# Five small padding tiles in a window-attention and two-MLP kernel: where the operands of its matrix products begin

## The chip, the cores and the metric

The kernel runs on one core of a Trainium2 chip. The metric is the device time of one execution in microseconds (us). Three executions were timed, and their median counts. TensorE multiplies; its two kinds of instruction stand in the rows as PE (the product, MATMUL) and PEld (the load of the stationary operand, LDWEIGHTS). DVE is VectorE, ACT ScalarE, POOL GpSimd. On-chip memory (SBUF) has 128 partitions; an address below is a byte offset in a partition.

## The reference

```python
# q, k, v: (4, 8, 576, 64); moe w_in (512, 2048), w_out (2048, 512), alpha (2048,); moe2 the same shapes
scores = scale * q @ k.T                      # with a bias -slope[h] * (i - j)
scores = where((i - j >= 0) & (i - j < 128), scores + bias, -1e9)
attn = softmax(scores) @ v                    # window of 128 keys
x = attn.transpose(0, 2, 1, 3).reshape(2304, 512)
h = x @ w_in;  g = max(h, 0) + alpha * min(h, 0);   x = g @ w_out
h = x @ w_in2; g = h * sigmoid(1.702 * h);          out = g @ w_out2
```

All in float32.

## The kernel before

TensorE works on the 4-byte type float32r. To keep float32 accuracy every operand a is split into a high part ah and a rest al, and a product a·b becomes three: ah·bh, ah·bl, al·bh, which add up in PSUM. Every one of them has a stationary operand of 128 partitions x 128 columns, which a LDWEIGHTS loads, and a moving operand of 256, 288 or 512 columns, which the MATMUL streams.

The program runs through five stretches.

- Start: first heads of the attention, and decoding of the first MLP's weights.
- Attention beside the first MLP. Tokens come in blocks of 256. `m1_h` (L579) multiplies a chunk of `w_in` (tiles wh, wl; stationary) with the tokens (tiles xh, xl; moving), 12 products of 256 columns for each of 16 hidden chunks and each of 7 blocks. `m1_o` (L625) multiplies `w_out` with the activations gh, gl, again 12 products for each chunk and block. Between them stand the small products of the attention: scores (L428, L429: stationary q, moving kh, kl), transposes (L492) and values (L530: stationary vp, moving pth, ptl), of 64 to 256 columns.
- The last two blocks go through the same two lines together, with 512 columns (the branch `k == KM`).
- The first product of the second MLP (L787), by a seven-product scheme on half matrices, with 288 columns.
- The second product of the second MLP (L884, `o_mm`), by a seven-product scheme too. Here the activations are stationary (tiles oh, ol) and the weights move (wh, wl), with 256 columns. It runs over 36 units (`quads`, a block of tokens and a pair of hidden chunks); unit number n keeps its activations in one of three tile pairs by n % 3: `oh0` on the left side of SBUF, `oh1` and `oh2` on the right side. A unit of a 512-token block has 42 products (7 x 2 x 3), one of the 256-token block 21.

The order of work is written out by hand in the lists of steps; the tile framework places tiles and semaphores. SBUF is filled from both ends by stacks of pools: a pool on the left side begins where the one opened before it ends, one on the right side ends where the one before it begins. A tile's address follows from the sizes of the pools opened before it and not from anything in its own line. The weight tiles (wh, wl) lie in a left pool opened early, at multiples of 256 bytes. Columns of 128 elements are 512 bytes wide, so all 128-column pieces of a tile have the same address modulo 256.

Of the kernel before, what the change touches and what calls it, by code (L numbers as in the profile page):

```python
# [11 lines left out]
F32 = mybir.dt.float32  # L12
F32R = mybir.dt.float32r
# [8 lines left out]
P = 128  # L22
# [47 lines left out]
def tile_window_attention__then__two_mlps(  # L70
# [20 lines left out]
    dram = ctx.enter_context(tc.tile_pool(name="dram", bufs=1, space=bass.MemoryType.DRAM))  # L91
    psh = ExitStack()
    ps_h = psh.enter_context(tc.tile_pool(name="ps_h", bufs=2, space=PSUM, side="right"))

    alph = const.tile([P, NF], F32, name="alph")
    beta = const.tile([P, NF], F32, name="beta")
# [32 lines left out]
    def w_load(i):  # L129
        layer, f, part = chunks[i]  # L130
        src = ((w_in1, w_out1), (w_in2, w_out2))[layer][part]
        s = wstage.tile([P, DM], I64, tag="ws", name="ws")
        nc.sync.dma_start(out=s, in_=src[f])
        wst[i] = s
# [92 lines left out]
    def w_out_diffs(p, half):  # L227
        c = DM // 2
        if half == 0:
            w0, w1 = wf.pop(("o", 2 * p)), wf.pop(("o", 2 * p + 1))  # L230
            t = stage_f32("sc").rearrange("p (i c) -> p i c", i=4)
            b11, b12, b21, b22 = w0[:, :c], w0[:, c:], w1[:, :c], w1[:, c:]
            tt(t[:, 0, :], b12, b11)
            tt(t[:, 2, :], b22, b12)
            wf["d", p] = t, b21, b22
        else:
            t, b21, b22 = wf.pop(("d", p))
            tt(t[:, 1, :], b22, t[:, 0, :])
            tt(t[:, 3, :], b21, t[:, 1, :])
            nc.sync.dma_start(out=wt2d[p], in_=t)  # L240

    def w_out_load(p):
        w = p2["wo"].tile([P, 2, DM], F32, tag="wo", name="wo")
        nc.sync.dma_start(out=w, in_=wo2d[p])
        if p < NPR - 2:
            t = stage_f32("st").rearrange("p (i c) -> p i c", i=4)
        else:
            t = p2["wo"].tile([P, 4, DM // 2], F32, tag="wo", name="wu")
        nc.sync.dma_start(out=t, in_=wt2d[p])
        wf["w", p] = w, t  # L250
# [54 lines left out]

    ps_o = ExitStack()
    pso = ps_o.enter_context(tc.tile_pool(name="ps_o", bufs=1, space=PSUM, side="right"))
    p1 = ExitStack()
    ring = p1.enter_context(tc.tile_pool(name="ring", bufs=1, side="right"))
    gp, gt, xsp = {}, {}, {}  # L310
# [8 lines left out]
    ap_ = at.enter_context(tc.tile_pool(name="att", bufs=1))  # L319
# [4 lines left out]
    ident = ap_.tile([P, P], F32, name="ident")  # L324
    relt = ap_.tile([P, 2 * P + 192], F32, name="relt")
    xps = ap_.tile([P, 320], F32, name="xp")
    ar = {x: ap_.tile([P, c], F32R, name=x) for x, c in (("q", 384), ("kh", 448), ("kl", 448))}

    af = ExitStack()
    apf = af.enter_context(tc.tile_pool(name="attf", bufs=1))  # L330
# [5 lines left out]
    def a_parts():  # L336
        af.close()
        pool = at.enter_context(tc.tile_pool(name="attr", bufs=1))
        for x, c in (("pth", 704), ("ptl", 640)):
            ar[x] = pool.tile([P, c], F32R, name=x)  # L340
        for i in range(2):
            ar["v", i] = pool.tile([P, 4, P], F32R, name=f"vp{i}")
        for x in ("pth", "ptl"):
            nc.gpsimd.memset(ar[x].bitcast(F32)[:, 384:448], 0.0)
# [308 lines left out]
    def x_load(j, c, key=None):  # L653
        r = stage_f32("xr", TB)
        done = 0
        while done < TB:
            i, o = divmod(j * TB + done, T1)
            m = min(T1 - o, TB - done)
            nc.sync.dma_start(out=r[:, done : done + m], in_=x2d[i][:, c, o : o + m])
            done += m  # L660
        xr[j, c if key is None else key] = r
# [366 lines left out]
    n = H + 2  # L1028
# [41 lines left out]
    halves, n = [], 2 * (H + 2)  # L1070
# [4 lines left out]
    for s, (k, f) in enumerate(steps):  # L1075
        n = H + 2 + s // 2
# [92 lines left out]
    def run():  # L1169
        while todo:  # L1170
            todo.pop(0)[2]()

    def task(fn, dve=0.0, act=0.0):
        todo.append((dve, act, fn))

    def dec_scale(f):
        task(lambda: w_scale(3 * NF + f), act=1.3)

    def dec_add(f):
        task(lambda: (w_shift(3 * NF + f), w_add(3 * NF + f), w_split(3 * NF + f)), 1.1)  # L1180

    def dec_tasks(i):
        task(lambda: w_scale(i), act=1.3)
        task(lambda: (w_shift(i), w_add(i), w_split(i)), dve=1.1)

    def x_tasks(j, cc):
        task(lambda: x_a(j, cc), 0.9, 0.4)
        task(lambda: (x_t12(j, cc), x_d3(j, cc), x_d4(j, cc)), 0.9, 0.65)
        task(lambda: x_lo(j, cc), 1.2)

    def win_tasks(p):
        box = []
        task(lambda: (box.extend(w_in_parts(p)), box[0]()), 1.3, 0.6)
        task(lambda: box[1](), 1.1, 0.4)
        task(lambda: box[2](), 0.4, 1.0)
        task(lambda: box[3](), 1.2)
# [19 lines left out]
    for d in range(NS // 2 + 1):  # L1216
        j, q = divmod(2 * d, NPR)
        q //= 2
        for i, (name, k) in enumerate(slots):
            s = 2 * d + k  # L1220
            if s < 0 or s >= NS:
                continue
            if (d, i) == (1, 0):
                run()
                for k in (2, 1):
                    w_load(W1 + NF - k)
                dec_tasks(W1 + NF - 2)
                win_tasks(6)
                dec_tasks(W1 + NF - 1)
            if (d, i) == (2, 0):  # L1230
                win_tasks(7)
            if j < NJ - 1:
                if (q, i) == (2, 2):
                    for c in (0, 2):
                        x_load(j + 1, c)
                if (q, i) == (2, 8):
                    x_tasks(j + 1, 0)
                if (q, i) == (3, 0):
                    for c in (1, 3):
                        x_load(j + 1, c)  # L1240
                if (q, i) == (3, 4):
                    x_tasks(j + 1, 1)
                if (q, i) == (3, 6):
                    for cc in range(2):
                        x_load(j + 1, cc + 2, f"b{cc}")
            if j in (1, 2):
                f = 2 + 4 * (j - 1) + q
                if i == 0:
                    dec_scale(f)
                if i == 4:  # L1250
                    dec_add(f)
                if i == 8 and f % 2:
                    task(lambda f=f: w_out_diffs(f // 2, 0), 0.85)
                    task(lambda f=f: w_out_diffs(f // 2, 1), 0.85)
                if i == 6 and f < 9:
                    w_load(3 * NF + f + 1)
            if (j, q, i) == (0, 3, 12):
                w_load(3 * NF + 2)
            if j == NJ - 1:
                if (q, i) == (1, 0):  # L1260
                    run()
                    px0.close()
                    p2["oh", 0] = ctx.enter_context(tc.tile_pool(name="oh0", bufs=1))
                    p2["wo"] = ctx.enter_context(tc.tile_pool(name="wo", bufs=2))
                if q and i in (0, 7):
                    w_out_load(2 * (q - 1) + i // 7)
                if q and i in (6, 9):
                    wout_tasks(2 * (q - 1) + (i - 6) // 3)
                if (q, i) == (1, 12):
                    o_load(*quads[0])  # L1270
                if (q, i) == (3, 0):
                    task(lambda: o_split(*quads[0]), 2.4, 2.0)
            h_mm(s, name)
            late.append(lambda s=s, name=name: h_post(s, name))
            if len(late) > 1:
                late.pop(0)()
            if (d, i) == (0, 2):
                for cc in range(2):
                    x_b(0, cc)
                for cc in range(2):  # L1280
                    x_b_lo(0, cc)
            if q == 0 and 0 < j < NJ:
                f = {0: (x_b_lo, 0), 1: (x_b_lo, 1), 2: (x_34, 3), 3: (x_34_lo, 3), 7: (x_34, 4), 8: (x_34_lo, 4)}.get(i)
                if f:
                    f[0](j, f[1])
            if q == 3 and j < NJ - 1 and i == 12:
                run()
                x_b(j + 1, 0)
            if q == 3 and j < NJ - 1 and i == 13:
                x_b(j + 1, 1)  # L1290
            credit = [min(c + 0.8 - t.get(name, 0.0), 2.4) for c, t in zip(credit, (PD, PA))]
            while todo and all(c >= min(x, 2.4) for c, x in zip(credit, todo[0][:2])):
                x = todo.pop(0)
                credit = [c - y for c, y in zip(credit, x[:2])]
                x[2]()
# [6 lines left out]
    p2["gs"] = ctx.enter_context(tc.tile_pool(name="gs", bufs=2, side="right"))  # L1302
    psh.close()
    p2["pr"] = ctx.enter_context(tc.tile_pool(name="ps_r", bufs=1, space=PSUM))
    for i in (1, 2):
        p2["oh", i] = ctx.enter_context(tc.tile_pool(name=f"oh{i}", bufs=1, side="right"))
    p3["o"] = ctx.enter_context(tc.tile_pool(name="ob", bufs=2, side="right"))
# [71 lines left out]
```

## Time and profile before

| | us |
|---|---|
| median of three runs | 915.97 (915.3 to 917.12) |
| span of the profiled execution, first to last instruction | 913.5 |
| median less span: what lies around the span | 2.5 |
| PE busy in the span | 896.6 (98%) |
| PEld busy | 861.0 (94%) |
| DVE busy | 715.3 (78%) |
| ACT busy | 582.7 (64%) |

The profile is of one execution; its own time is the span plus what lies around it, and 2.5 us is put for that, from the median. A MATMUL's busy time is longer than the distance to the next one, since products overlap in the pipeline; what a product costs in a full stream is the distance from its start to the next start, called its spacing below.

### The profile page before, as it was taken

The page shows a single profiled execution, that of the slowest core. Times are in us where ns is not written, and L with a number is a line of the kernel's source. Part 1 is how long each engine was busy: PE and PEld are TensorE (multiplying, and loading weights), DVE is VectorE, ACT ScalarE, POOL GpSimd, SP SyncE. Part 2 cuts the span into 40 slices and gives each one's busy share as a digit, 9 for nine tenths or more (in the row PEclk, how much of TensorE's full clock was granted, in tenths as well). Part 3 has the DMA queues.
Part 4 walks back from the last instruction along what each step waited for, and adds up shares of the span by engine and source line. Part 5 has one row for each costly group of instructions (what it writes and reads, how often), then busy time and mean ns, then how long its engine had stood idle before and what let it go on. Part 6 is the DMA issues. An engine that isn't in the chain of part 4 may idle for free.

```text
span 913.5 us, 19339 instructions
## 1 busy us (share of the span) xinstructions
PE 896.6 (98%) x6882; PEld 861.0 (94%) x6884; DVE 715.3 (78%) x1906; ACT 582.7 (64%) x1459; POOL 91.1 (10%) x127
## 2 busy tenths in 40 slices
PE   7799999999999999999999999999999999999998
PEld 3589899999999999999988889999999999999998
DVE  5998877779988889888857777656665689878875
ACT  5999766667777777777645556555557754433432
POOL 1100112122222222222100000000000000000000
PEclk8999999999999999999999999999999999999999
DMA  8776412223424334235023325757668873544423
GB/s 230 235 229 214 158 58 58 79 85 99 149 86 141 104 87 154 75 92 149 18 81 128 93 73 171 226 177 249 237 234 288 302 256 106 164 137 118 145 63 93
DMA packets 73585, 133.43 MB, mean 146 GB/s; under 512 B 14224, under 2 KB 32656, under 8 KB 73488
## 3 DMA queue, kind: packets, MB, share of 16 engines
q1 hardware_dynamic: 73488, 132.19, 45.9%
q8 instruction: 54, 0.88, 0.4%
q14 instruction: 43, 0.35, 0.1%
HBM read 95.46 MB, written 36.70 MB: 145 GB/s over the span
## 4 chain that ended last, share of the span: by engine, by line
PE 94%; DMA 2%; ACT 2%; DVE 2%; issue 0%; SPq 0%; DVEq 0%; ACTq 0%
PE h L579 22%; PE p L884 19%; PE o L625 17%; PE p L787 14%; PE h L787 6%; PE p L625 5%; PE x L530 3%; PE pt L492 3%; PE s L429 2%; PE s L428 2%; DMA raw<-in_u_dram 2%; PE s L419 1%; DMA ws<-in_w_out_dram 1%; PE x L518 1%; ACT ws L147 0%
## 5 line engine op out<-in xcount | busy, mean ns | idle before, releaser
L579 PE MATMUL h<-xh,wh 128*128 128x256 f32 (+1 forms) x512 | 152.5, 300 | 3.3 <-ACT xh L565 2.7
L579 PE MATMUL h<-xl,wh 128*128 128x256 f32 (+1 forms) x512 | 152.2, 298 | 0.5 <-DVE xl L109 0.5
L579 PE MATMUL h<-xh,wl 128*128 128x256 f32 (+1 forms) x512 | 152.3, 298 | 0.2 <-DVE wl L109 0.2
L884 PE MATMUL p<-wl,oh 128*128 128x256 f32 x504 | 138.3, 280 | 0.0
L884 PE MATMUL p<-wh,oh 128*128 128x256 f32 x504 | 137.1, 281 | 0.3 <-ACT oh L104 0.3
L884 PE MATMUL p<-wh,ol 128*128 128x256 f32 x504 | 133.2, 280 | 0.0
L625 PE MATMUL o<-gl,wh 128*128 128x256 f32 x448 | 126.3, 283 | 0.0
L625 PE MATMUL o<-gh,wl 128*128 128x256 f32 x448 | 125.5, 282 | 0.0
L625 PE MATMUL o<-gh,wh 128*128 128x256 f32 x448 | 124.8, 284 | 0.0
L579 PEld LDWEIGHTS h<-xh,wh 128*128 128x128 f32 x512 | 96.2, 189 | 7.7 <-ACT xh L565 4.0
L579 PEld LDWEIGHTS h<-xl,wh 128*128 128x128 f32 x512 | 96.6, 189 | 3.5 <-DVE xl L109 0.7
L579 PEld LDWEIGHTS h<-xh,wl 128*128 128x128 f32 x512 | 96.6, 189 | 3.3 <-DVE wl L109 0.4
L884 PEld LDWEIGHTS p<-wl,oh 128*128 128x128 f32 x504 | 95.2, 189 | 0.0
L884 PEld LDWEIGHTS p<-wh,oh 128*128 128x128 f32 x504 | 94.3, 189 | 0.5 <-ACT oh L104 0.5
L884 PEld LDWEIGHTS p<-wh,ol 128*128 128x128 f32 x504 | 92.1, 189 | 0.0
L625 PEld LDWEIGHTS o<-gl,wh 128*128 128x128 f32 x448 | 84.5, 189 | 0.1
L625 PEld LDWEIGHTS o<-gh,wl 128*128 128x128 f32 x448 | 84.5, 189 | 0.0
L625 PEld LDWEIGHTS o<-gh,wh 128*128 128x128 f32 x448 | 83.4, 189 | 0.8 <-issue 0.7
L593 ACT ACTIVATE n<-h 128x256 f32<-128x256 f32 (+1 forms) x128 | 51.6, 405 | 48.9 <-PE h L579 47.6
L455 ACT ACTIVATE tt<-tt,st 128x192 f32<-128x192 f32 (+2 forms) x160 | 74.6, 469 | 9.8 <-DVE st L439 9.8
L104 ACT CAST oh<-gs 128x1024 fp32r<-128x1024 f32 (+1 forms) x40 | 38.0, 962 | 66.1 <-issue 30.0
L599 DVE SCALAR_TENSOR_TENSOR g<-n,beta,h 128x256 f32<-128x256 f32 x112 | 53.3, 476 | 15.0 <-ACT n L593 13.3
(154 smaller groups left out, 2382.3 us busy)
## 6 DMA issues: line engine op xcount, KB each, us to landing
g2d<-G SPq DMA_DIRECT2D x64, 288.0 KB, 2.9
ws<-in_w_in_dram SPq DMA_DIRECT2D x32, 512.0 KB, 4.0
ws<-in_w_out_dram SPq DMA_DIRECT2D x32, 512.0 KB, 4.6
gr<-g2d SPq DMA_DIRECT2D x32, 512.0 KB, 4.4
raw<-in_u_dram SPq DMA_DIRECT2D x32, 352.0 KB, 3.0
raw<-in_u_dram SPq DMA_DIRECT2D x16, 320.0 KB, 2.9
raw<-in_u_dram SPq DMA_DIRECT2D x32, 160.0 KB, 2.3
xr<-x2d SPq DMA_DIRECT2D x40, 128.0 KB, 2.7
```

Of the source, the lines that this page charges most:

```text
L104: return nc.scalar.copy(o, i)
L428: nc.tensor.matmul(o[:, :n_], q, kh[:, ks : ks + n_], start=True, stop=False)
L429: nc.tensor.matmul(o[:, :n_], q, kl[:, ks : ks + n_], start=False, stop=True)
L455: nc.scalar.activation(t, t, AF.Exp, bias=s[:rows, i : i + 1], scale=-1.0, accum_out=s[:rows, 4 + i : 5 + i])
L492: nc.tensor.transpose(banks[bank][:, dst : dst + P], src, ident)
L530: nc.tensor.matmul(x[:, oc : oc + nq], v, p[:, col : col + nq], start=(i == 0 and k == 0), stop=(i == len(js) - 1 and k == (j < 4)), skip_ ...
L579: nc.tensor.matmul(ph, w[:, 0, c * P : (c + 1) * P], x[:, c, r : r + n], start=(c == 0 and i == 0), stop=(c == NC - 1 and i == 2),)
L593: nc.scalar.activation(n, ph, AF.Relu, scale=-1.0)
L599: nc.vector.scalar_tensor_tensor(g, n, beta[:, f : f + 1], ph, op0=ALU.mult, op1=ALU.add)
L625: nc.tensor.matmul(o, w[:, 1, c * P : (c + 1) * P], g, start=(first and (k == KM or c % 2 == 0) and i == 0), stop=(last and i == 2), skip_ ...
L787: tc.keep_in_program_order(nc.tensor.matmul(o, w[:, cc * P : (cc + 1) * P], x[:, h, cc, i, :], start=first and cc == 0 and k == 0, stop=la ...
L884: mm = nc.tensor.matmul(o[:, m, :], g[:, a, m * P : (m + 1) * P], w, start=(p == 0 and m == 0 and i == 0), stop=(p == NF // 2 - 1 and i == 2),
```

## The change

Five pieces of SBUF that nothing reads or writes are put in: 32 bytes per partition on the right side ahead of the token tiles, 192 between q and kh, 64 between ptl and vp, 64 on the left side ahead of `oh0`, 128 on the right side ahead of `oh1` and `oh2`.

```diff
+    def shift(stack, n, side="left"):
+        stack.enter_context(tc.tile_pool(name="pad", bufs=1, side=side)).tile([P, n // 4], F32, name="pad")
...
     pso = ps_o.enter_context(tc.tile_pool(name="ps_o", bufs=1, space=PSUM, side="right"))
+    shift(ctx, 32, "right")
     p1 = ExitStack()
     ring = p1.enter_context(tc.tile_pool(name="ring", bufs=1, side="right"))
...
-    ar = {x: ap_.tile([P, c], F32R, name=x) for x, c in (("q", 384), ("kh", 448), ("kl", 448))}
+    ar = {"q": ap_.tile([P, 384], F32R, name="q")}
+    ap_.tile([P, 48], F32, name="padk")
+    ar |= {x: ap_.tile([P, 448], F32R, name=x) for x in ("kh", "kl")}
...
             ar[x] = pool.tile([P, c], F32R, name=x)
+        pool.tile([P, 16], F32, name="padv")
         for i in range(2):
             ar["v", i] = pool.tile([P, 4, P], F32R, name=f"vp{i}")
...
                     px0.close()
+                    shift(ctx, 64)
                     p2["oh", 0] = ctx.enter_context(tc.tile_pool(name="oh0", bufs=1))
...
     p2["pr"] = ctx.enter_context(tc.tile_pool(name="ps_r", bufs=1, space=PSUM))
+    shift(ctx, 128, "right")
     for i in (1, 2):
         p2["oh", i] = ctx.enter_context(tc.tile_pool(name=f"oh{i}", bufs=1, side="right"))
```

No instruction is added, removed or moved, and no semaphore changes: on all five engines the two programs have the same list of instructions with the same operands' names, shapes and waits. What differs is where tiles lie. The table gives, from the addresses in the two built programs, the **offset** of a product: the address of its moving operand less that of its stationary operand, modulo 256.

| products | columns | count | moving / stationary address mod 256 before | offset before | after |
|---|---|---|---|---|---|
| L579, tokens xh, xl | 256 | 1344 | 224 / 0 | 224 | 192 |
| L625, activations gh, gl | 256 | 1344 | 224 / 0 | 224 | 192 |
| L884, units in `oh0` | 256 | 525 | 0 / 0 | 0 | 192 |
| L884, units in `oh1`, `oh2` | 256 | 987 | 0 / 224 | 32 | 192 |
| L428, L429, L530 (attention) | 256 | 256 | 128 / 128 | 0 | 192 |
| the same lines | 64 to 192 | 288 | 128 / 128 | 0 | 192 |
| L579, last two blocks | 512 | 192 | 224 / 0 | 224 | 192 |
| L625, last two blocks | 512 | 192 | 0 / 0 | 0 | 0 |
| L787, tiles on the right side | 288 | 528 and 528 | 224 / 0 and 96 / 0 | 224 and 96 | 192 and 64 |
| L787, tiles on the left side | 288 | 144 and 144 | 0 / 0 and 128 / 0 | 0 and 128 | 0 and 128 |

## Rows read from the trace of the kernel before

**Rows 1.** The page: busy time by engine; the chain that ended last, by engine.
```profile
PE 896.6 (98%) x6882; PEld 861.0 (94%) x6884; DVE 715.3 (78%) x1906; ACT 582.7 (64%) x1459; POOL 91.1 (10%) x127
...
PE 94%; DMA 2%; ACT 2%; DVE 2%; issue 0%; SPq 0%; DVEq 0%; ACTq 0%
```
**Rows 2.** Waits of PE: total us, times, longest.
```profile
PE h L579 <- ACT xh L565: 2.7, 3, 1.4
PE pt L492 <- DVE tt L479: 2.4, 1, 2.4
PE x L518 <- ACT pt L499: 2.3, 5, 0.7
```
**Rows 3.** Instruction groups of PE by shape: count, busy us, mean ns, idle before.
```profile
L884 PE MATMUL p<-wh,oh 128*128 128x256 f32 x504 | 137.1, 281 | 0.3 <-ACT oh L104 0.3
...
L579 PE MATMUL h<-xl,wh 128*128 128x256 f32 x448 | 126.7, 284 | 0.5 <-DVE xl L109 0.5
...
L625 PE MATMUL o<-gh,wh 128*128 128x256 f32 x448 | 124.8, 284 | 0.0
...
L579 PE MATMUL h<-xh,wl 128*128 128x512 f32 x64 | 25.3, 395 | 0.0
```
**Rows 4.** Windows of whole stretches: start:end, length, busy us, clock, DMA.
```profile
76.00:227.00 151.00, 149.65 (x1254) 147.88 (x1254) 118.54 (x375) 109.08 (x328) 28.42 (x44) 1.00 0.33 102
227.00:464.00 237.00, 237.00 (x2021) 236.59 (x2019) 207.69 (x668) 173.62 (x508) 53.88 (x56) 1.00 0.34 103
464.00:545.00 81.00, 81.00 (x360) 66.20 (x359) 58.29 (x104) 46.08 (x80) 0.00 (x0) 1.00 0.34 105
545.00:730.00 185.00, 185.00 (x1374) 183.70 (x1374) 118.82 (x250) 116.74 (x254) 0.00 (x0) 1.00 0.68 231
730.00:913.50 183.50, 179.10 (x1517) 178.67 (x1515) 150.43 (x314) 75.54 (x135) 1.47 (x2) 1.00 0.45 136
```
**Rows 5.** The chain in time, pieces of 256 columns: start, us, what.
```profile
439.95 1.42 PE o L625 x12
...
444.03 1.42 PE o L625 x12
...
457.36 1.42 PE h L579 x12
```
**Rows 6.** Windows over L884 alone, two times one and two units: busy PE, PEld.
```profile
820.18:825.21 5.03, 5.03 (x45) 5.03 (x43) 1.00 0.18 32
825.21:835.01 9.80, 9.80 (x86) 9.80 (x85) 1.00 0.46 147
835.02:840.05 5.03, 5.03 (x45) 5.03 (x43) 1.00 0.70 195
840.05:849.85 9.80, 9.80 (x86) 9.80 (x85) 1.00 0.24 65
```
**Rows 7.** The chain in time, pieces of 512 and 288 columns.
```profile
469.42 5.13 PE h L579 x22
...
544.28 8.19 PE p L625 x36
...
574.76 3.18 PE p L787 x24
```
**Rows 8.** Timeline of PE among attention products: start, us, what.
```profile
430.10 0.25 PE L530 MATMUL x<-pth,vp 128*128 128x192 f32 x1
430.19 0.28 PE L530 MATMUL x<-ptl,vp 128*128 128x192 f32 x1
430.31 0.27 PE L530 MATMUL x<-pth,vp 128*128 128x192 f32 x1
430.41 0.31 PE L579 MATMUL h<-xh,wh 128*128 128x256 f32 x1
```
**Rows 9.** Timeline of PEld in the same stretch.
```profile
430.11 0.19 PEld L530 LDWEIGHTS x<-ptl,vp 128*128 128x128 f32 x1
430.21 0.19 PEld L530 LDWEIGHTS x<-pth,vp 128*128 128x128 f32 x1
430.33 0.19 PEld L579 LDWEIGHTS h<-xh,wh 128*128 128x128 f32 x1
430.44 0.19 PEld L579 LDWEIGHTS h<-xl,wh 128*128 128x128 f32 x1
```

## The prediction

> **What bounds the kernel now.** The page comes first [rows 1]. PE is busy for 98% of the span, and the chain that ended last lies on PE for 94%. DVE has 78%, ACT 64%. The next view is who PE waits for [rows 2]: the longest entry is 2.7 us in three waits, so hardly anything can be won from waits. What is left is the stream of products itself. The groups by shape [rows 3] show what it consists of: products of 256 columns at L579 (three groups of 448), at L625 (three of 448) and at L884 (three of 504), 4200 in all, and beside them the groups of 512 columns. A product's mean of 281 to 284 ns is no price, because products overlap; the price is the spacing, and it has to be read from stretches where PE never pauses. The windows [rows 4] say where these are: from 76 to 464 us, from 464 to 545 and from 545 to 730 PE is busy for all but 1.4 us, at granted clock 1.00, which is 2.4 GHz. At 2.4 GHz a column takes 1/2.4 ns, so 256 columns take 106.7 ns, if one column enters per clock.
>
> Now the spacing that the trace has. Twelve products of L625 or of L579 in a row take 1.42 us [rows 5], which is 118.3 ns each. Their offset is 224. For L884 the windows [rows 6] hold whole units, and by the program's order the windows of 5.03 us are a unit in `oh0` and those of 9.80 us the two units in `oh1` and `oh2` (the counts 45 and 86 hold some products still running at the edges). So offset 0 costs 5.03 / 42 = 119.8 ns and offset 32 costs 9.80 / 84 = 116.7 ns, with the same line, the same shapes, the same moving tiles and PE never idle. It comes back to the same hundredth in the second pair of windows, with the DMA share at 0.18, 0.46, 0.70 and 0.24, in no order with the spacing. So where the operands begin does change the spacing, by 3.1 ns of 118. This is the row on which the forecast rests. All products of 256 columns stand 10 to 13 ns above the 106.7 ns, 4200 x 11.4 = 48 us together, and that is the pool that the change draws on.
>
> **The change part by part.** It adds no instruction and no wait, and no queue changes; the padding itself costs nothing, since nothing writes or reads it, and space is not scheduled. All of it acts through the offset. 192 has no product of 256 columns in this trace, so its spacing q is bounded from both sides.
>
> From above: 119.8 ns, the highest level that a full stream of this shape shows [rows 6]. From below: the weight loads. Where the products have only 192 columns, 80 ns of streaming, three of them start 90, 120 and 100 ns apart [rows 8], and the load sets the pace: beside them the loads start at 430.11, 430.21, 430.33 and 430.44, 0.33 / 3 = 110 ns apart [rows 9]. A product of 256 columns with a load each can't come faster than the loads do, so 110 is the floor. Between the ends lie two nearer readings. From offset 0 to 224, 32 bytes down, the spacing falls from 119.8 to 118.3; the same step again, to 192, gives 116.8. And 116.7 is a level that is reached already, at 32. The middle of 110 and 116.8 is 113.4; I take **q = 115**, on the side of the levels that have been seen.
>
> - L579 and L625, 256 columns: 2688 x (118.3 - 115.0) ns = 8.9 us.
> - L884 in `oh0`: 525 x (119.8 - 115.0) = 2.5 us.
> - L884 in `oh1`, `oh2`: 987 x (116.7 - 115.0) = 1.7 us.
> - L579 with 512 columns, 224 to 192: 5.13 / 22 = 233.2 ns now, where L625 of the same shape has 8.19 / 36 = 227.5 at offset 0 [rows 7]. Half of that distance, 192 x 2.85 = 0.5 us; bounds nothing and 1.1 us.
> - L787, 288 columns: 3.18 / 24 = 132.5 ns [rows 7]. 1056 products move by 32, but their two offsets alternate, and no row parts them. I put 0; by the whole spread of the 256 shape, 3.1 ns, it is at most 3.3 us either way.
> - The attention's products: the shorter ones go at the pace of the loads [rows 9] and gain nothing; 256 of 256 columns move from 0 to 192, at most 256 x 4.8 = 1.2 us; put at 0.
> - Operands of DVE and ACT on the right side move by the same 32 to 192 bytes. Neither sets the end, and no row shows a dependence; 0.
>
> Sum 13.6 us. Against it stands what becomes a wait. From 76 to 464 us DVE is busy 118.5 + 207.7 of 388 us [rows 4], 84%; with 8.9 us less it is 86%. DVE's work there hides under PE, so the gain passes through nearly whole, but the waits on xh and pth of [rows 2] should grow a little. I take off 1.0 us; if DVE or ACT held that stretch at its present length the loss would be all of the 8.9. In the last stretch DVE has 150.4 of 183.5 us, 82%, and the same holds. So 12.6 us: a span of 900.9 and with the 2.5 us around it **903.4 us**. The span and the runs agree by that constant alone (913.5 + 2.5 = 916.0).
>
> **A rule that speaks against it.** The windows [rows 6] have two levels for the same instruction, 119.8 and 116.7 ns, which differ by the stationary tile's place alone. The Trainium skill, in "TensorE: Matmul & The Clock Gate", section "Step-by-step: what each phase is for", says that PE has two independent read ports into SBUF, one for the moving operand and one for LDWEIGHTS, and that a load for the next tile takes no read bandwidth from the running matmul. By that rule no placing could matter, and the sum would be 0 and the time 916. The trace does not agree as far as the 3.1 ns go, and no run here tells yet whether ports or something behind them are shared.
>
> **The rivals.**
>
> *Nothing measurable (916 us).* The 3.1 ns in [rows 6] come not from the offset but from the side of SBUF or from the sum of both addresses, and moving tiles by 32 bytes at L579 and L625 changes nothing; L884 gains 1.5 and loses about as much. For it: 224 and 32 differ by 1.6 ns though both are 32 from 0, so the offset alone isn't a distance. Against it: four levels out of three placements are stable to a tenth of a ns. The rule above would end here too.
>
> *The floor (884 to 892 us).* The spacing falls to that of the loads. At 110 ns: 2688 x 8.3 + 525 x 9.8 + 987 x 6.7 = 34.1 us, with 0.5 for the 512 columns and 2.6 us of new waits 32 us, so 884; at 112 ns 892. For it: PEld's busy share is 94%, and its pace in [rows 9] is close. Against it: nothing in the trace has 256 columns at that spacing.
>
> *Slower (923 us).* The load for the next product runs beside the whole of the streaming, and 192 lets the two meet more often than 224 did. The place is L579 and L625, 2688 of the 4200. For it: the 512 columns have it the other way round (233.2 at 224, 227.5 at 0), so one shape's order of offsets is not the other's, and 224 isn't known to lie on a slope that keeps falling. At the worst level seen, 119.8: 2688 x 1.5 + 987 x 3.1 = 7.1 us. The point from which it decides is the mean spacing now, (2688 x 118.3 + 525 x 119.8 + 987 x 116.7) / 4200 = 118.1 ns: above it the kernel is slower.
>
> **How the numbers follow.** A measurement of this kernel can tell about 0.2%, 1.8 us, which is 0.44 ns of spacing over 4200 products. A q from 113 to 117 is the forecast, chance 0.50, own range 895 to 912. The floor, q below 113, 0.14. Nothing measurable, q from 117.7 to 118.5, 0.16. Slower, 0.20. So faster 0.64, same 0.16, slower 0.20. The range of 8 in 10 runs from 890, within the floor's 884 to 892, to 922, just short of the worst level's 923; it leaves out some 0.07 below and 0.10 above.
>
> **What will show it.** In the profile after, twelve products of L579 or L625 in a row should take 1.36 to 1.40 us and not 1.42; one unit in `oh0` 4.83 instead of 5.03, and two in the others 9.66 instead of 9.80, so that all three placements have one spacing. If L884 has one spacing and L579 another, the offset isn't the cause. The stretch up to 464 us should be shorter by about 8 us, the last by about 4, and the one of L787 unchanged. If PE's waits on DVE or ACT grow by several us, the gain was real and lost there. The forecast is wrong if q is above 117.7.

## The result

The changed kernel takes 901.93 us, median of five runs (901.32 to 903.59), against 917.0 for the kernel before in the same five rounds (915.3 to 917.18). The ratio is 0.9842, with a 95% interval of 0.9829 to 0.9856: 1.6% faster, about 14.5 us by the ratio and 15.1 between the two medians. The forecast was 903.4, its range 890 to 922.

Lines have moved by a few: L579 is now L586, L625 is L632, L787 is L794 and L884 is L891. The page's busy times and the chain answer to [rows 1]:

```profile
PE 885.6 (98%) x6882; PEld 848.9 (94%) x6884; DVE 715.6 (79%) x1906; ACT 581.9 (65%) x1459; POOL 91.5 (10%) x127
...
PE 94%; ACT 2%; DMA 1%; DVE 1%; issue 0%; SPq 0%; POOL 0%; ACTq 0%; DVEq 0%
```

PE has lost 11 us of busy time with the same 6882 instructions; DVE and ACT are as before. The shares have not moved: PE is still the bound.

Windows over L891, one unit of 42 products and the next two, in the same form as [rows 6]:

```profile
820.92:825.68 4.76, 4.76 (x45) 4.76 (x43) 1.00 0.35 106
825.68:835.20 9.52, 9.52 (x87) 9.52 (x85) 1.00 0.38 113
```

4.76 / 42 and 9.52 / 84 are 113.3 ns, where [rows 6] gave 119.8 and 116.7. All three tile pairs have one spacing here. (L891 has 40 units, not 36 as said above: 32 of 42 products and, in the last block, eight of 21.) At 2.4 GHz 113.3 ns are 272 clocks, 16 more than the 256 columns; the levels before are 280 and, to a fraction, 288.

The same stretches of work as in [rows 4]; each window begins and ends at the same place in the program:

```profile
227.00:458.70 231.70, 231.70 (x2017) 231.29 (x2016) 207.40 (x666) 172.24 (x508) 53.84 (x56) 1.00 0.34 105
458.70:539.60 80.90, 80.90 (x359) 65.95 (x358) 58.30 (x105) 46.06 (x80) 0.00 (x0) 1.00 0.33 105
539.60:724.50 184.90, 184.90 (x1375) 183.65 (x1374) 118.85 (x250) 116.78 (x254) 0.00 (x0) 1.00 0.67 231
724.50:901.80 177.30, 172.91 (x1516) 172.46 (x1514) 150.18 (x314) 75.34 (x135) 1.47 (x2) 1.00 0.46 142
```

The first stretch of [rows 4] ended at 464.00 and ends now at 458.70, 5.3 us earlier; the second takes 80.9 us for 81.0 and the third 184.9 for 185.0, so they gave nothing; the last takes 177.3 for 183.5, 6.2 us less. The two profiled executions differ by 11.7 us (913.5 and 901.8) and the medians of the runs by 15.1, because the profile of before was one of its shorter executions and that of after the longest of its five (spans 899.5 to 901.8). In the fourteen traces of this case (before, after and the twelve experiments) what varies lies mostly in the start. The 301st product of 256 columns of the line of `m1_h` begins between 133.3 and 137.7 us, in no order with its offset; in the four kernels that have 192 there and in the attention (the changed one, e7, e8 and e10) it is 133.4 to 136.4. From there to the first product of 512 columns behind them the work takes 318.37 us in every one of these four, and 325.05 in before and in e2, where the offset is 224. So the stretches behind the start can be compared between single traces, and the start can't.

The chain in time shows the shape that did not move, 512 columns, as in [rows 7]:

```profile
464.00 5.13 PE h L586 x22
...
538.84 8.18 PE p L632 x36
```

Offset 192 costs L586 the same 233 ns there as 224 did.

### The profile page after: what moved, and what is told of

The parts are those of the page before. It is cut to its first block, busy times and chain, and to the rows that moved or that the text cites. A ratio compares the mean times of both kernels' runs of the same rounds, so it can differ in the third digit from the quotient of the medians.

```text
span 901.8 us, 19339 instructions
## 1 busy us (share of the span) xinstructions
PE 885.6 (98%) x6882; PEld 848.9 (94%) x6884; DVE 715.6 (79%) x1906; ACT 581.9 (65%) x1459; POOL 91.5 (10%) x127
## 4 chain that ended last, share of the span: by engine, by line
PE 94%; ACT 2%; DMA 1%; DVE 1%; issue 0%; SPq 0%; POOL 0%; ACTq 0%; DVEq 0%
PE h L586 22%; PE p L891 19%; PE o L632 17%; PE p L794 14%; PE h L794 6%; PE p L632 5%; PE x L537 3%; PE pt L499 3%; PE s L436 2%; PE s L435 2%; DMA raw<-in_u_dram 1%; PE s L426 1%; PE x L525 1%; ACT tt L462 0%; DVE wl L112 0%
## 5 line engine op out<-in xcount | busy, mean ns | idle before, releaser
L586 PE MATMUL h<-xh,wh 128*128 128x256 f32 (+1 forms) x512 | 152.1, 299 | 3.3 <-ACT xh L572 2.7
L586 PE MATMUL h<-xl,wh 128*128 128x256 f32 (+1 forms) x512 | 151.7, 297 | 0.5 <-DVE xl L112 0.5
L586 PE MATMUL h<-xh,wl 128*128 128x256 f32 (+1 forms) x512 | 151.4, 296 | 0.2 <-DVE wl L112 0.2
L891 PE MATMUL p<-wl,oh 128*128 128x256 f32 x504 | 136.2, 276 | 0.0
L891 PE MATMUL p<-wh,oh 128*128 128x256 f32 x504 | 135.0, 277 | 0.3 <-ACT oh L107 0.3
L891 PE MATMUL p<-wh,ol 128*128 128x256 f32 x504 | 131.0, 276 | 0.0
L632 PE MATMUL o<-gl,wh 128*128 128x256 f32 x448 | 124.7, 280 | 0.0
L632 PE MATMUL o<-gh,wl 128*128 128x256 f32 x448 | 124.0, 278 | 0.0
L632 PE MATMUL o<-gh,wh 128*128 128x256 f32 x448 | 123.5, 281 | 0.0
L586 PEld LDWEIGHTS h<-xh,wh 128*128 128x128 f32 x512 | 96.9, 190 | 7.8 <-ACT xh L572 4.0
L586 PEld LDWEIGHTS h<-xl,wh 128*128 128x128 f32 x512 | 97.3, 190 | 3.6 <-DVE xl L112 0.7
L586 PEld LDWEIGHTS h<-xh,wl 128*128 128x128 f32 x512 | 97.2, 190 | 3.3 <-DVE wl L112 0.4
L891 PEld LDWEIGHTS p<-wl,oh 128*128 128x128 f32 x504 | 94.6, 188 | 0.0
L891 PEld LDWEIGHTS p<-wh,oh 128*128 128x128 f32 x504 | 93.7, 188 | 0.5 <-ACT oh L107 0.5
L891 PEld LDWEIGHTS p<-wh,ol 128*128 128x128 f32 x504 | 91.4, 188 | 0.0
L632 PEld LDWEIGHTS o<-gl,wh 128*128 128x128 f32 x448 | 84.4, 188 | 0.1
L632 PEld LDWEIGHTS o<-gh,wl 128*128 128x128 f32 x448 | 84.4, 188 | 0.0
L632 PEld LDWEIGHTS o<-gh,wh 128*128 128x128 f32 x448 | 83.2, 188 | 0.8 <-issue 0.3
L794 PE MATMUL p<-xt,wh 128*128 128x288 f32 x320 | 64.6, 295 | 0.0
```

What stands on the lines that cost most here:

```text
L586: nc.tensor.matmul(ph, w[:, 0, c * P : (c + 1) * P], x[:, c, r : r + n], start=(c == 0 and i == 0), stop=(c == NC - 1 and i == 2),)
L632: nc.tensor.matmul(o, w[:, 1, c * P : (c + 1) * P], g, start=(first and (k == KM or c % 2 == 0) and i == 0), stop=(last and i == 2), skip_ ...
L794: tc.keep_in_program_order(nc.tensor.matmul(o, w[:, cc * P : (cc + 1) * P], x[:, h, cc, i, :], start=first and cc == 0 and k == 0, stop=la ...
L891: mm = nc.tensor.matmul(o[:, m, :], g[:, a, m * P : (m + 1) * P], w, start=(p == 0 and m == 0 and i == 0), stop=(p == NF // 2 - 1 and i == 2),
```

## The experiments

All of them are the changed kernel with other pads, unless the text says otherwise. A spacing given without a window is the mean distance from a product's start to the next one's in the trace, over the unbroken part of a line. The offsets of each experiment come from the addresses in its built program. e3, e4 and e6 to e11 are single runs; what is read from them is the spacing in their traces and not their time.

**The parts alone.** The first keeps only the 32 bytes on the right side, the second only the pads ahead of L891's tiles, the third only the two of the attention.

```diff
 # e1: only this line of the change
+    shift(ctx, 32, "right")
 # e2: only these
+                    shift(ctx, 64)
+    shift(ctx, 160, "right")
 # e12: only these
+    ap_.tile([P, 48], F32, name="padk")
+        pool.tile([P, 16], F32, name="padv")
```

> Only the 32 bytes on the right side are put in, not the four other pads. Offsets: L579 and L625 192, as in the changed kernel; L884 0 in the first tile pair as before, and 64 in the two others. Theory (the spacing of a product of 256 columns depends on the offset): L579 and L625 at about 115 ns as in the changed kernel, L884 in the first pair at 119.8 as before, and a level of its own for offset 64; 2688 x 3.3 = 8.9 us less than before, so about 907 us. Rival (the place in SBUF counts, not the offset): the first pair's level moves although its offset does not, or L579 and L625 stay at 118.3 and the time at 916.

> Only the pads ahead of the three activation pairs of L884 are put in (64 on the left, 160 on the right), so all of L884 has offset 192 and L579 and L625 keep 224. Theory: L884 at 113.7 ns as in the changed kernel, L579 and L625 at 118.3 as before; 525 x 6.1 + 987 x 3.0 = 6.2 us less than before, about 910 us. With the run of the right-hand 32 bytes alone the two gains should add to the whole 15 us. Rival (part of the gain comes from elsewhere, the attention's tiles or the engines that feed TensorE): the two parts together stay clearly below 15 us.

> Only the two pads of the attention (192 bytes ahead of kh, 64 ahead of the vp tiles): the attention's 544 products of float32r go from offset 0 to 192, all else stays at its offset of before. Prediction's own term: nothing, at most 1.2 us, so 916 to 917 us, no change that can be told. Rival (the small products between the large ones set how these settle): L579 and L625 leave 118.2 ns although their own offset is 224, and the time moves by more than 2 us.

| | time, us | before beside it | ratio (95%) | first MLP, 256 columns | second MLP, last product |
|---|---|---|---|---|---|
| e1 | 906.34 | 916.79 | 0.9888 (0.9873 to 0.9903) | 114.9 and 114.6 | 119.9 at offset 0, 113.8 at 64 |
| e2 | 910.93 | 916.79 | 0.9964 (0.9939 to 0.9990) | 118.1 and 118.2 | 113.7 |
| e12 | 917.32 | 915.94 | 1.0008 (0.9996 to 1.0020) | 118.2 and 118.3 | 119.6 at 0, 116.8 at 32 |

By the runs the gains are 1.12%, 0.36% and none. They are not parts that add up to the 1.58% of the whole, since e1 moves two of the three tile pairs of the last product too, to 64, and gains there. The traces part them. The first column goes from the 301st product of 256 columns of `m1_h` to the first of 512 columns behind them, the second from the first product of L891 (L888 in e1, L887 in e2 and e12) to the end of the span:

| | first MLP, us | last product, us |
|---|---|---|
| before | 325.05 | 186.1 |
| e1 | 319.1 | 183.4 |
| e2 | 325.05 | 180.2 |
| e12 | 325.2 | 186.2 |
| changed kernel | 318.4 | 180.1 |

So the 32 bytes on the right give 6.0 us in the first MLP, the pads ahead of L891's tiles 6.0 us in the last product, and 0.7 us more comes in the first MLP of the changed kernel, whose attention stands at 192 and not at 0 as in e1: 12.7 of the 12.8 us that the two stretches gain together. e12 shows that the attention's pads give nothing beside an offset of 224. In these three experiments each line takes the level of its own offset. In e2, L887 shows the windows of the changed kernel:

```profile
820.80:825.56 4.76, 4.76 (x44) 4.76 (x43) 1.00 0.67 208
825.56:835.08 9.52, 9.52 (x86) 9.52 (x85) 1.00 0.52 148
```

**The map of offsets.** Three kernels give the four places other offsets. The four numbers of each are the bytes of its pads; a is e3, b is e4 and c is e6.

```diff
-    shift(ctx, 32, "right")
-                    shift(ctx, 64)
-    shift(ctx, 128, "right")
+    # right side, ahead of oh0, of oh1, of oh2: a 64, 192, 0, 32; b 96, 96, 96, 32; c 224, 224, 192, 224
```

> Same pads with other sizes: offset 160 for L579 and L625, and 64, 96 and 128 for the three pairs of L884. Theory (offset, with the worst case where both operands begin in the same place modulo 256 and better ones farther away): all four lie below 118 ns, and 64 has the same level as in the run with the right-hand 32 bytes alone, although there its tile pair lies on the other side. Rival (192 is one good value among bad ones): some of them lie above 118. Rival (side of SBUF): 64 on the left reads otherwise than 64 on the right.

> Same pads with other sizes: offset 128 for L579 and L625, and 160, 224 and 0 for the three pairs of L884; the pair with offset 0 lies on the right side here, and 0 and 224 are offsets whose levels are known from other places. Theory (offset): 0 on the right side costs 119.8 ns as it did on the left, 224 in L884 costs 118.3 as it did at L579 and L625, 160 about what it costs at L579 in the other map. Rival (side or line): 0 on the right is not 119.8, or L884 at 224 differs from 118.3 by more than 1 ns.

> Pads sized for offset 0 at L579 and L625, and 32, 192 and 160 in the three pairs of L884; 32 lies on the left here, 192 between units of other offsets. Theory (offset alone): L579 and L625 at 119.8 ns, L884 at 116.7, 113.7 and 118.0, whatever stands before. Rival (side or history): 32 on the left, or 192 between units of other offsets, leaves its level by more than 1 ns. L579 with 512 columns stands at offset 0 for the first time: if its 233 ns came from the offset it falls to the 228 of L625, otherwise it stays.

| offset | last product, ns | first MLP (L586, L632), ns |
|---|---|---|
| 0 | 119.6 (before), 119.9 (e1), 119.7 (e4, right side) | 119.5 (e6) |
| 32 | 116.8 (before), 116.8 (e6, left side) | |
| 64 | 113.8 (e1), 117.8 (e3) | |
| 96 | 119.8 (e3) | |
| 128 | 118.7 (e3) | 119.1 (e4) |
| 160 | 118.0 (e4), 119.8 (e6) | 117.9 (e3) |
| 192 | 113.7 (after), 114.4 (e6) | 114.9 (after) |
| 224 | 118.5 (e4) | 118.2 (before) |

The times of these single runs are 919.76, 917.03 and 916.32 us. The side of SBUF doesn't count: 0 and 32 read the same on either side. 192 is not one of many good offsets; 0, 96, 128, 160 and 224 lie between 117.9 and 119.9. So the theory of e3, that all its four lie below 118, is wrong for 96 and 128. Offset 64 reads two ways, 4 ns apart, with the same addresses modulo 256, and 160 differs by 1.8, against the theories of e3 and e6 that the offset alone decides; that called for runs of its own, below. And the 512 columns do have their own order: with L586 at offset 0 (e6) the chain shows 5.01 / 22 = 227.7 ns, the level of L632, where the changed kernel has 5.13 / 22:

```profile
472.82 5.01 PE h L586 x22
...
546.29 8.16 PE p L632 x36
```

**Where both begin.** All left-hand tiles, the weights among them, begin 32 bytes later, and the right side is set so that the offset stays 192.

```diff
+    ctx.enter_context(tc.tile_pool(name="padw", bufs=1)).tile([P, 8], F32, name="padw")
     wpool = ctx.enter_context(tc.tile_pool(name="w", bufs=1))
...
-    shift(ctx, 32, "right")
```

> The offset is 192 everywhere as in the changed kernel, but the weights and all that goes with them begin 32 bytes later, so that stationary and moving operands begin at odd multiples of 32. Theory (only the difference of the two addresses counts): L884 at 113.7 ns, L579 and L625 at about 115, time 902 us. Rival (it counts that both operands begin at a multiple of 64): L884 and the others above 116 ns, time above 910.

902.87 us, and the windows of L891 are those of the changed kernel:

```profile
820.19:824.95 4.76, 4.76 (x44) 4.76 (x43) 1.00 0.35 108
824.95:834.47 9.52, 9.52 (x86) 9.52 (x85) 1.00 0.40 113
```

Both operands begin at odd multiples of 32, and the spacing is the same: for this step of 32 bytes it is the difference that counts. The rival of a 64-byte alignment falls.

**Finer than 32.** Slices that begin 8 or 16 bytes inside the tile; the pads ahead of `oh1` and `oh2` become 160 and 224 (left out here).

```diff
+        k = (4, 4, 2)[quads.index((j, p)) % 3]
-        gh, gl = (p2["oh", quads.index((j, p)) % 3].tile([P, 7, HALF], F32R, tag=f"o{x}", name=f"o{x}") for x in "hl")
+        gh, gl = (
+            p2["oh", quads.index((j, p)) % 3].tile([P, 7 * HALF + 64], F32R, tag=f"o{x}", name=f"o{x}")[
+                :, k : k + 7 * HALF
+            ].rearrange("p (i t) -> p i t", i=7)
+            for x in "hl"
+        )
```

> The changed kernel with the three pairs of L884 at offsets 176, 208 and 184 in place of 192, by slices that begin 8 or 16 bytes inside a tile; L579 and L625 stay at 192. Theory (192 is the foot of a valley some 32 wide on either side, since 160 reads 118 to 120 and 224 118): all three lie between 113.5 and 118, and none below 113.3. Rival (the least lies between the steps of 32): one of them is below 113 ns and worth a kernel of its own.

The expectation of a valley is wrong. Three units in a row, at 184, 176 and 208:

```profile
867.48:872.45 4.97, 4.97 (x44) 4.97 (x43) 1.00 0.25 58
872.45:877.45 5.00, 5.00 (x45) 5.00 (x44) 1.00 0.32 100
877.45:882.60 5.15, 5.15 (x44) 5.15 (x43) 1.00 0.21 54
```

That is 118.3, 119.0 and 122.6 ns, 908.6 us in all. Eight bytes beside 192 nearly all of the gain is gone in this kernel, and no better offset turned up. That 192 is a sharp point is not shown by it, for two reasons. No unit here follows one of its own offset or of 192, and what ran before can count (below). And the stationary tiles begin at 80, 48 and 72 modulo 256, which are no multiples of 32 as in all other kernels here, so their own start may count and not the distance from 192.

**Own load or next load.** In two of the tile pairs oh and ol begin at different places; the pad ahead of `oh2` becomes 32 (left out here).

```diff
+        pool = p2["oh", quads.index((j, p)) % 3]
-        gh, gl = (p2["oh", quads.index((j, p)) % 3].tile([P, 7, HALF], F32R, tag=f"o{x}", name=f"o{x}") for x in "hl")
+        gh = pool.tile([P, 7, HALF], F32R, tag="oh", name="oh")
+        if n_pad[quads.index((j, p)) % 3] and quads.index((j, p)) < 3:     # n_pad = (192, 64, 0)
+            pool.tile([P, n_pad[quads.index((j, p)) % 3] // 4], F32, tag="padl", name="padl")
+        gl = pool.tile([P, 7, HALF], F32R, tag="ol", name="ol")
```

> In L884 the high and the low parts of the activations begin at different places: in the first pair offset 192 for oh and 0 for ol, in the second 0 for oh and 192 for ol, in the third 32 for both; L579 and L625 at 192 as in the changed kernel. The products come in threes: wh with oh, wl with oh, wh with ol. Theory O (a product's own load and its own stream meet): in the first pair the products on oh take about 113.5 ns and those on ol 120, in the second the other way round. Theory N (the load for the next product runs under this product's stream, so the next one's stationary address counts): in the first pair the second product of three, which has ol next, takes 120 and the others 113.5; in the second pair the second takes 113.5 and the others 120.

906.93 us. Units of the second, third and first pair:

```profile
816.81:821.76 4.95, 4.95 (x45) 4.95 (x43) 1.00 0.70 195
821.76:826.66 4.90, 4.90 (x44) 4.90 (x43) 1.00 0.28 99
826.66:831.62 4.96, 4.96 (x45) 4.96 (x44) 1.00 0.67 196
```

Neither theory: the two mixed units take 117.9 and 118.1 ns a product, and the three kinds of product in them lie within 1.2 ns of each other (first pair 118.5, 118.6 and 117.6). A product at 192 between products at 0 is no faster than these; all kinds stand 1 to 2 ns below the 119.8 of a run at 0 and 4 to 5 above the 113.3 of a run at 192. So 113.3 ns is not a property of one product and its own offset: it came only where products of one offset follow each other.

**What ran before.** First all 256-column products at 64, then the same kernel with only the left pair moved to 0, then to 128.

```diff
+    # right side, ahead of oh0, of oh1, of oh2: e5 160, 192, 128, 0; e9 160, 0, 128, 0; e11 160, 128, 128, 0
```

> The pads are sized so that all 256-column products of L579, L625 and L884 have offset 64 in place of 192. Known so far: offset 64 costs 113.8 ns on the right side after units of offset 0, and 117.8 ns on the left side between units of 128 and 96. Theory A (history: with this offset the stream can settle at either spacing, and what ran before decides): the left pair, now between units of the same offset, reads 113.8 too, and the time is near that of the changed kernel, 902 us. Theory B (side of SBUF): left 117.8, right 113.8. If L579 and L625 read 118 everywhere, 192 is better than 64 where short products cut in, and the time is about 910.

> The kernel with offset 64 everywhere, but its left pair of L884 at offset 0: only the left pad is taken out, the two right pairs lie where they lay and keep 64. Theory H (history: at 64 the stream can hold two spacings, and what ran before a unit decides): the right pairs, which now come after units of offset 0, read 113.8 ns as in the run with the right-hand 32 bytes alone, not the 117.8 that they had when all was 64. Rival (something else differed in that run, such as the place of the other engines' tiles): the right pairs stay at 117.8.

> As the run with 64 after 0, but the left pair of L884 at offset 128; again only the left pad differs. Theory H: the right pairs after units of 128 read 117.8 ns, as the pair with 64 did that came between units of 128 and 96. Rival: they read the same as after units of offset 0.

Three units in a row of L891, the left pair first, in e5, e9 and e11:

```profile
829.15:834.09 4.94, 4.94 (x44) 4.94 (x43) 1.00 0.70 199
834.09:839.04 4.95, 4.95 (x44) 4.95 (x43) 1.00 0.09 20
839.04:843.99 4.95, 4.95 (x45) 4.95 (x43) 1.00 0.37 107
```
```profile
829.31:834.35 5.04, 5.04 (x45) 5.04 (x44) 1.00 0.72 193
834.35:839.11 4.76, 4.76 (x45) 4.76 (x44) 1.00 0.09 23
839.11:843.87 4.76, 4.76 (x45) 4.76 (x43) 1.00 0.41 109
```
```profile
833.53:838.52 4.99, 4.99 (x45) 4.99 (x43) 1.00 0.68 196
838.52:843.47 4.95, 4.95 (x45) 4.95 (x44) 1.00 0.09 21
843.47:848.41 4.94, 4.94 (x44) 4.94 (x43) 1.00 0.35 110
```

The second and third units have the same tiles at the same addresses in all three kernels. After a unit at 0 they run at 113.3 ns, after one at 64 or 128 at 117.8, and they keep it through both units. The left pad moves two buffers besides `oh0`, but in these traces they were last read at 759 to 764 us. History decides, as theory H had it; that the left pair of e5 would read 113.8 was wrong, and so was its theory of sides, as left and right both read 117.8. e5 took 910.85 us, ratio 0.9934 (0.9911 to 0.9957), e9 908.45 and e11 913.98. At 64, in e5, L632 shows both states within a few us. They alternate with the two patterns of attention products ahead of it, 1.36 us behind scores and 1.41 behind values:

```profile
431.33 1.36 PE o L632 x12
434.89 1.41 PE o L632 x12
438.93 1.36 PE o L632 x12
```

Offset 192 has the same two levels. In e6 its whole units follow units at 32 and take 113.8 ns with the change-over, and in the changed kernel 1363 products of L891 in a row keep 113.3. But the last 105, from 885.18 us on, take 117.8 with the offset unchanged, and in e2 and e7 the last 106. Two windows of 42 products each of the changed kernel, ahead of the change and behind it:

```profile
880.42:885.18 4.76, 4.76 (x45) 4.76 (x43) 1.00 0.84 264
887.66:892.60 4.94, 4.94 (x44) 4.94 (x43) 1.00 0.19 56
```

What starts the slower spacing there was not tried. So 64 and 192 differ not in their levels but in which of the two their streams took: at 64 everywhere L891 stayed at 117.8, at 192 everywhere it stayed at 113.3 nearly to the end. The offset of the unit before is not all of the history either: in e10 the whole units at 208, each behind one at 176, read 117.8, 118.4 or 122.7. No version here beats the changed kernel.

## Why the prediction was right

**The bound and the mechanism.** Right. PE carries the whole gain, the instructions are the same, and where the operands begin changes the spacing, on either side of SBUF and from either starting address (e4, e6, e7). The prediction gave each offset one spacing, though, and that is not so: 64, 160 and 192 have more than one (e4, e6, e9, e11 and the changed kernel itself). The rival of nothing measurable is out, and so is the slower one. The slower one was not far off as a reading, though: six of the eight multiples of 32 have a level of about 117 to 120, and the 512 columns do go the other way, as it held.

**q = 115 at 192.** In L891 it is 113.3 in a settled stream and 113.7 with the edges, in L586 and L632 114.7 to 115.2 outside of interruptions. The number came out right and the way to it did not, so it was luck. I read 119.8, 118.3, 116.8 as a slope in steps of 32 bytes; the map shows no slope, with 117.9 to 119.8 at 160 on the other side of 192. It was luck too that the stream at 192 held the faster of its two levels; at the slower, 117.8, the forecast would have been wrong by its own sign of q above 117.7. The floor from the weight loads, 110 ns, did its work as a bound: 113.3 is as near as any steady stream here came.

**The sum.** It was 12.6 us and the profiled pair shows 11.7, but two terms were mis-sized and nearly cancel. L891 was put at 2.5 + 1.7 = 4.2 us and gave 6.2 [rows 4], since its spacing is 113.3 and not 115. L579 and L625 were put at 8.9, less the 1.0 of waits, and that stretch gave 5.3. The step that failed there is the count: all 2688 products were priced as if in a full stream. 2088 of them lie in the stretch from the 301st such product of L586 to the 512 columns; at the predicted 3.3 ns each they would give 6.9 us, and the same work takes 318.4 us against 325.0, as the windows of the two kernels show (before, then after):

```profile
135.10:460.10 325.00, 325.00 (x2781) 325.00 (x2780) 276.29 (x889) 235.16 (x700) 72.79 (x83) 1.00 0.32 97
```
```profile
136.40:454.80 318.40, 318.40 (x2782) 318.40 (x2781) 276.22 (x889) 234.29 (x700) 72.77 (x83) 1.00 0.32 99
```

All 6.6 us come from there. The other 600 products, nearly all ahead of that stretch and put at 2.0 us, show no gain: up to its start the changed kernel was even 1.3 us later in this execution, within the 133.3 to 137.7 us at which that product begins in the kernels here. What holds the start back was not tried. The growth of PE's waits did not come: PE still waits 2.7 us for xh.

Inside the full stream the level of L586 and L632 is 1 to 2 ns above the settled one. Most of what raises it are the products right behind the attention's. From the second large product to the fourth the spacing is 117.5 to 116.6 ns, at the fifth 114.7, and from the sixth to the twentieth about 113.8; in the kernel before it shows no such fall, at about 118 throughout. The chain shows it where the settled pieces begin late:

```profile
430.43 0.95 PE h L586 x8
431.38 1.36 PE o L632 x12
432.74 0.55 PE x L537 x5
433.29 0.61 PE h L586 x5
```

0.95 / 8 = 119, then 1.36 / 12 = 113.3, then 0.61 / 5 = 122.

**The small terms.** L794 with 288 columns, put at nothing: right, 184.9 for 185.0 us, and from its first product to L891's it takes 174.8 to 175.8 us in all fourteen traces. The attention, put at nothing and at most 1.2 us: e12 alone shows no change, and beside an offset of 192 it is the 0.7 us above. The 512 columns of L586, 0.5 us: nothing came, since only offsets 0 and 64 are lower there (about 227 and 230 ns), and 128 to 224 all read 233.0 to 233.7.

**The rule of two ports.** By the section of the Trainium skill named in the prediction, as the prediction read it, the placing could not matter; with 113.3, 116.7 and 120 ns for the same instruction the trace does not agree. The runs show that the spacing depends on where the moving operand begins against the stationary one, and that a state of the stream persists. That the stream and the loads disturb each other is the likely reading; which part of the memory or of the engine they would share, no run here shows.

## What to carry to other kernels

When TensorE is busy without a pause, divide a window by its count of products and compare the spacing with the columns' own time; if two places with the same shape differ by a few per cent, look at the addresses of both operands before anything else. Measure the offsets, one tile pair each in a stage that repeats, rather than reading a trend from two or three; and let a candidate follow other offsets as well as its own, since it may keep a state that it inherits. Cost a gain per product only for those products that lie in a full, settled stream.

## What the hardware showed that was not expected

- A gain can vanish within 8 bytes: at 192 a product of 256 columns takes 113.3 ns, at 184 it took 118.3, at 176 119.0, at 208 118 to 123. Whether the offset, its neighbours or a start that is no multiple of 32 did it is open.
- The stream has more than one steady spacing with the same instructions and addresses: 113.3 or 117.8 ns at offset 64, held for two whole units of 42 products and chosen by the unit before; and the same two at 192, 113.3 for 1363 products and then 117.8 for the last 105.
- The number of columns has its own order of offsets: for 512 columns 0 is best (about 227 ns) and 192 among the worst (233.3), for 256 the reverse (119.6 and 113.3).
